# Reordered weight requests, column-tile runs, score slots and output products in a fused windowed-attention and gated feed-forward kernel

## The chip, the cores and the metric

The kernel runs on one core of one Trainium2 chip. The metric is the device time of one execution, in microseconds (us). The time before is the median of three runs.

The core's engines are named as in the profile: PE is TensorE (matrix products), PEld its weight loads, ACT ScalarE, DVE VectorE, POOL GpSimd, SP SyncE. SP, ACT and POOL also ask for transfers. All engines run side by side, each through its own list of instructions in order, and wait for one another by semaphores.

## What is computed

Attention in which each query sees the first four keys ("sinks") and the last 128, and then a gated feed-forward layer on the joined heads.

```python
batch, n_heads, seq, head_dim = (4, 8, 768, 64);  n_sink, window = (4, 128)
scores = scale * np.matmul(q, k.transpose(0, 1, 3, 2))
keep = is_sink | in_window
a = softmax(np.where(keep, scores, -1e9))          # shortened
x = np.matmul(a, v)          # heads joined: 3072 tokens x 512
gate = np.maximum(x @ w_gate, 0.0)                 # 512 x 1536
val = x @ w_val                                    # 512 x 1536
out = gate * val @ w_out                           # 1536 x 512
```

All inputs and the output are float32 in memory. The kernel computes in bfloat16 and sums in float32.

## The kernel before

The kernel treats the four batches one after the other, and for each batch four pairs of heads. A pair of heads in a batch is a unit; units 0 to 3 are batch 0, units 4 to 7 batch 1, and so on. The work of TensorE is laid out in 96 slots, 24 for each batch. A slot holds one chunk of the feed-forward layer: four products for the gate and four for the value, for one of 12 column tiles m of 128, and for one of two halves g of the batch's tokens.

```python
for ko in range(KO):                                  # 4: the gate, L356
    nc.tensor.matmul(out=gp[:, 0:n], lhsT=wg[:, ko, m * 128:(m + 1) * 128], rhs=x[:, ko, c], ...)
nc.scalar.activation(gs[:, 0:n], gp[:, 0:n], Act.Relu, ...)                       # L359
for ko in range(KO):                                  # the value, L361
    nc.tensor.matmul(out=vp[:, 0:n], lhsT=wv[:, ko, m * 128:(m + 1) * 128], rhs=x[:, ko, c], ...)
nc.vector.tensor_tensor(h[:, m, c], gs[:, 0:n], vp[:, 0:n], op=Alu.mult)          # L363
```

Batch 0 goes through its chunks in two runs: tiles 0 to 8 of half 0, then of half 1, then tiles 9 to 11 of both. The other batches have a single run of 12 tiles for each half.

```python
for b, runs in enumerate((((0, 9), (9, FM)),) + ((((0, FM),),) * (B - 1))):
    slots += [(b, g, m) for m0, m1 in runs for g in range(2) for m in range(m0, m1)]
```

After its chunk, a slot has pieces of attention of the same or the next batch, named by letters and a unit in the plans:
- T (L254 to L259): the casted keys and queries of a unit are turned on TensorE, copied out of PSUM, and the keys of the odd tiles are copied once more beside them (L185, and the four sink keys, L181). H is the same for half a unit of batch 0.
- S (L290, L294, L296): scores of one of three groups of key tiles, the exponential on ScalarE, and the mask on VectorE.
- W (L321, L326, L327): probabilities times V, and the division by the sum.
- X (L338, L341): the result is turned into xT, the input of the chunks.

For batches 2 and 3, T and X are done by transfers instead: cast, write to memory, and a transposing read back.

The second product of the feed-forward layer (L388) follows in pieces: one output tile of 128 tokens takes 12 products, one for each column tile. They all go to PSUM bank G[3] until the tail, where three banks rotate. After the twelfth, ScalarE copies the tile out (L392).

```python
OP = [[G[3][:]], [G[3][:], PP[0][:, 0, :], PP[1][:, 0, :]]]
...
nc.tensor.matmul(out=op, lhsT=hT[b % 2][:, m, t * 128:(t + 1) * 128], rhs=wo[:, m, :], start=m == 0, stop=m == FM - 1)
if m == FM - 1:
    ot = outpool.tile([128, d_model], F32, name="ot")
    nc.scalar.copy(ot[:], op)                                                     # L392
    nc.sync.dma_start(out=out[...], in_=ot[:])
```

The list of these products is filled at the end of slot 23. Slot 23 takes some of them at once (F8 and F5 in its plan: 13), and each later slot takes three:

```python
for _ in range(3 if s > 23 else 0):
    if f2:
        f2.popleft()()
```

Weights are asked for from GpSimd, with a cast to bfloat16 on the way: `load_w(m0, m1)` asks for tiles m0 to m1 of both weights, `load_w(m0, m1, (1,))` for those of w_val alone. GpSimd also casts keys, queries and V to bfloat16, and does so in the order of the program. `prep[s]` lists what is given to GpSimd and SyncE ahead of slot s: ("half", c) and ("kq", i) cast keys and queries, ("v", b, j) casts one tile of V, ("load", i) asks for a unit's keys and queries (for units 4 to 6 only once ScalarE has come to that slot), ("lv", b) for a batch's V, ("w", ...) and ("wo",) for weights.

```python
prep[1] += [("half", 6), ("half", 7), ("w", 6, 8), ("setup3",), ("v", 0, 3), ("v", 0, 4), ("v", 0, 5), ("v", 0, 6),
            ("w", 8, 10)]
prep[7] += [("load", 4), ("load", 5), ("load", 6)]
prep[9] += [("kq", 4), ("load", 7), ("lv", 1)]
prep[10] += [("kq", 5), ("w", 10, 12)]
prep[12] += [("kq", 6)]
prep[13] += [("kq", 7)]
prep[14] += [("v", 1, 0), ("v", 1, 1), ("v", 1, 2), ("v", 1, 3), ("wo",), ("v", 1, 4), ("v", 1, 5), ("v", 1, 6)]
```

Of the kernel before, what the change touches and what calls it, by code (L numbers as in the profile page):

```python
# [21 lines left out]
def kernel(  # L22
# [12 lines left out]
    nc = tc.nc  # L35
    B, H, S, D = q.shape
# [5 lines left out]
    FM = d_ff // 128  # L42
# [65 lines left out]
    half = lambda bufs, c: bufs[c // 2 % len(bufs)][:, c % 2 * HALF:c % 2 * HALF + HALF]  # L108
# [7 lines left out]
    def cast_half(c, copies=(nc.gpsimd.tensor_copy, nc.gpsimd.tensor_copy)):  # L116
        for src, dst, copy in ((kf, kn, copies[0]), (qf, qn, copies[1])):
            copy(half(dst, c).rearrange("p (n h d) -> p h n d", n=3, h=2),
                                  half(src, c).rearrange("p (h n d) -> p h n d", n=3, h=2))
# [13 lines left out]
    def cast_v(b, j, rows=128, copy=nc.gpsimd.tensor_copy):  # L133
        copy(vn[b % 2][0:rows, j, :, 0:64], vf[0:rows, j, :, :])  # L134
# [44 lines left out]
    def sinks(u, copy):  # L179
        e = kE[u.i % NT]  # L180
        copy(odd(e)[:, :, 0:4], e[:, 0:4].unsqueeze(1).to_broadcast([128, 3, 4]))  # L181

    def odd_tiles(u, copy):
        e = kE[u.i % NT]
        copy(odd(e)[:, :, 4:128], e[:, 120:876].rearrange("d (i c) -> d i c", c=252)[:, :, 0:124])  # L185
        sinks(u, copy)

    def load_w(m0, m1, which=(0, 1)):
        for w, dst in (((moe_w_gate, wg), (moe_w_val, wv))[x] for x in which):
            nc.gpsimd.dma_start(out=dst[:, :, m0 * 128:m1 * 128],  # L190
                                in_=w.rearrange("(ko ki) n -> ki ko n", ki=128)[:, :, m0 * 128:m1 * 128])
# [47 lines left out]
    def pair():  # L239
        rot[0] += 1  # L240
        return PP[rot[0] % 2]
# [6 lines left out]
    def T(u):  # L248
        t = u.i % NT
        tk, tq = G[3][:], pair()[:, 0, :]  # L250
        for x, ps in ((kn[u.i % 2], tk), (qn[u.i % 2], tq)):
            for n in range(NR):
                c = slice(128 * n, 128 * n + 128)
                nc.tensor.transpose(ps.bitcast(BF16)[:, c], x[:, c], ident[:])  # L254
        vk, vq = (ps.bitcast(BF16)[:, 0:S].rearrange("d (n p) -> d p n", p=128) for ps in (tk, tq))
        e = kE[t]
        to = lambda ap: ap.rearrange("d (p n) -> d p n", n=NR)
        nc.scalar.copy(to(e[:, 0:S]), vk)
        (nc.scalar.copy if u.p < 2 else nc.vector.tensor_copy)(to(qT[t]), vq)  # L259
        odd_tiles(u, nc.vector.tensor_copy)  # L260

    def T_half(c, banks=None):
        t, x = c % NP, c // NP
        tk, tq = banks or (G[3][:, 0:256], G[3][:, 256:512])
        for src, ps in ((kn, tk), (qn, tq)):
            for n in range(3):
                nc.tensor.transpose(ps.bitcast(BF16)[:, 128 * n:128 * n + 128], half(src, c)[:, 128 * n:128 * n + 128],  # L267
                                    ident[:])
        vk, vq = (ps.bitcast(BF16)[:, 0:HALF].rearrange("d (n p) -> d p n", p=128) for ps in (tk, tq))
        e = kE[t]  # L270

        for r0, r1, c0 in (((0, 128, 0), (40, 82, ODD + 4), (124, 128, ODD + 140)) if x == 0 else
                           ((0, 128, HALF), (0, 38, ODD + 152), (80, 122, ODD + 276))):
            nc.scalar.copy(e[:, c0:c0 + 3 * (r1 - r0)].rearrange("d (p n) -> d p n", n=3), vk[:, r0:r1])  # L274
        (nc.scalar.copy if c == 4 else nc.vector.tensor_copy)(
            qT[t][:, x * HALF:x * HALF + HALF].rearrange("d (p n) -> d p n", n=3), vq)
        if x == 0:
            sinks(U[t], nc.scalar.copy)
# [116 lines left out]
    with tc.manual_schedule():  # L395
# [22 lines left out]
        Sg(U[1], 3)  # L418
        cast_half(3)
        T_half(3, (g[0], g[1]))  # L420
        for j in range(3):
            cast_v(0, j)
        load_w(0, 2, (1,))
        load_w(2, 4)
        Sg(U[2], 0)
        Sg(U[2], 3)
# [19 lines left out]

        slots = []

        for b, runs in enumerate((((0, 9), (9, FM)),) + ((((0, FM),),) * (B - 1))):
            slots += [(b, g, m) for m0, m1 in runs for g in range(2) for m in range(m0, m1)]  # L450
        plan = [[] for _ in slots]
        at = {}
# [1 line left out]
        def put(s, y, n):  # L454
            st = (y[0], n * NP + int(y[1]), int(y[2]) if len(y) > 2 else 0)
            at[st] = s
            plan[s].append(st)

        for s, w in {0: "H0", 1: "S04 H1", 2: "S02 H2 S14", 3: "S12 H3", 4: "S24 S22", 5: "S34 S32", 6: "W01",
                     7: "W11 X01 W21", 8: "X11 W31 X21 X31"}.items():  # L460
            for y in w.split():
                put(s, y, 0)
        for s, w in {11: "T0", 12: "T1", 13: "S00 S01", 14: "S02 S10", 15: "T2 S11", 16: "S12 T3", 17: "S20 S21",
                     18: "S22 W0", 19: "S30 X0", 20: "S31 W1", 21: "S32 X1", 22: "W2", 23: "W3 X2 F8 X3 F5"}.items():
            for y in w.split():
                if y[0] == "F":
                    plan[s].append(("F", int(y[1:]), 0))
                else:
                    put(s, y, 1)
        for b, sl in ((2, {25: "S00 S01", 27: "S02 S10", 29: "S11 S12", 31: "S20 S21", 32: "W0", 33: "S22 S30",  # L470
# [3 lines left out]
            for s, w in sl.items():  # L474
                for y in w.split():
                    put(s, y, b)
        prep = [[] for _ in slots]
        prep[1] += [("half", 6), ("half", 7), ("w", 6, 8), ("setup3",), ("v", 0, 3), ("v", 0, 4), ("v", 0, 5), ("v", 0, 6),
                    ("w", 8, 10)]
        prep[7] += [("load", 4), ("load", 5), ("load", 6)]  # L480
        prep[9] += [("kq", 4), ("load", 7), ("lv", 1)]
        prep[10] += [("kq", 5), ("w", 10, 12)]
        prep[12] += [("kq", 6)]
        prep[13] += [("kq", 7)]
        prep[14] += [("v", 1, 0), ("v", 1, 1), ("v", 1, 2), ("v", 1, 3), ("wo",), ("v", 1, 4), ("v", 1, 5), ("v", 1, 6)]
        for i, ts in ((8, (13, 17, 18, 20)), (9, (14, 18, 19, 21)), (10, (15, 20, 21, 23)), (11, (19, 21, 22, 25)),
                      (12, (28, 31, 33, 36)), (13, (30, 33, 35, 38)), (14, (32, 35, 37, 42)), (15, (34, 37, 39, 43))):
# [13 lines left out]
        for s, (b, g, m) in enumerate(slots):  # L501
# [38 lines left out]
            for what, i, x in plan[s]:  # L540
                if what == "F":
                    for _ in range(i):
                        f2.popleft()()
                elif what == "X":
                    X(U[i], x if i < NP else None)
                elif what == "T":
                    T(U[i])
                elif what == "H":
                    T_half(NP + i)
                elif what == "S":  # L550
                    Sg(U[i], x)
                else:
                    W(U[i], x if i < NP else None)
# [43 lines left out]
```

The softmax here doesn't subtract the row's maximum and nothing guards it: scores larger than these inputs give would overflow.

## Time and profile before

| | before |
|---|---|
| time, median of three runs | 280.89 us (280.35 to 284.46) |
| profiled run, and its span from first to last instruction | 286.93 us, 285.0 us |
| PE busy | 244.7 us (86%) |
| DVE, ACT, POOL busy | 120.9, 120.8, 67.9 us |
| mean granted clock of PE | 0.974 |
| moved by DMA | 40.07 MB, mean 141 GB/s |

How to read it: the span is shown in 40 slices of 7.1 us, with one digit for each engine, the busy share in tenths. PEclk is the clock granted to TensorE, in tenths of full speed. A wait line names an engine and line, then what released it, then the total of those waits in us, their number and the longest. A line of a timeline has start, length, engine, line, operation, tiles, shape and count, and in brackets the idle time before it and its releaser. An engine's idle time costs something only where other work then comes later, in the end the last instruction; here TensorE has by far the most work.

### The profile page before, as it was taken

Reading aid. Unit: us, or ns where it says so; the run is one execution under the profiler, and the core shown is the slowest. Engines: PE = TensorE matmul, PEld = TensorE weight load, DVE = VectorE, ACT = ScalarE, POOL = GpSimd, SP = SyncE. Lnnn points to the kernel's source line nnn. Section 1 sums busy time; section 2 is a strip of 40 time slices with the busy share of each in tenths; the row PEclk is TensorE's granted clock in tenths of the full one; section 3 lists DMA queues with packets and bytes.
Section 4 is the critical chain, followed back from the end, with each engine's and each line's share of the span. In section 5 each row is a group of like instructions: output and inputs, shape, how many; then the busy total and the mean of one; then the engine's idle time right before and its main releaser. Section 6 shows DMA issues by size and latency. Waiting matters only on the chain.

```text
span 285.0 us, 5299 instructions
## 1 busy us (share of the span) xinstructions
PE 244.7 (86%) x2063; PEld 141.4 (50%) x2084; DVE 120.9 (42%) x227; ACT 120.8 (42%) x222; POOL 67.9 (24%) x120
## 2 busy tenths in 40 slices
PE   7869825997899978879889988978998988988895
PEld 3445523565466544546444545545554444544443
DVE  5466830379665335564322544645222222222100
ACT  4748711497473546452223645442222322222221
POOL 6895433099252126023004400000000000000000
PEclk9999985899799999999999999999999999999999
DMA  7999599799999834599997410231411000010113
GB/s 221 256 238 185 106 286 292 161 317 212 284 220 192 193 94 166 173 276 207 173 224 172 94 39 37 62 96 36 112 48 39 37 37 3 37 38 37 39 74 110
DMA packets 76737, 40.07 MB, mean 141 GB/s; under 512 B 53544, under 2 KB 73768, under 8 KB 76712
## 3 DMA queue, kind: packets, MB, share of 16 engines
q1 hardware_dynamic: 67560, 34.10, 47.0%
q0 software_dynamic: 7920, 4.72, 11.8%
q10 hardware_dynamic: 1232, 0.92, 1.0%
q8 instruction: 16, 0.26, 0.4%
q14 instruction: 9, 0.07, 0.1%
HBM read 28.48 MB, written 11.25 MB: 139 GB/s over the span
## 4 chain that ended last, share of the span: by engine, by line
PE 67%; DMA 13%; ACT 7%; SPq 5%; DVE 4%; issue 3%; POOL 1%; ACTq 0%; POOLq 0%; DVEq 0%
PE g L361 19%; PE g L388 19%; PE g L356 18%; DMA vf<-in_v_dram 5%; DMA wv<-in_moe_w_val_dram 4%; ACT ot L392 4%; PE pp L321 4%; DMA qf<-in_q_dram 4%; PE pp L290 3%; SPq L131 3%; ACT ee L294 3%; PE pp L388 2%; DVE xn L327 1%; DVE ee L296 1%; SPq L113 1%
## 5 line engine op out<-in xcount | busy, mean ns | idle before, releaser
L363 DVE TENSOR_TENSOR hT<-gs,g 128x384 bf16<-128x384 f32 (+2 forms) x96 | 53.0, 552 | 116.7 <-PE g L361 112.9
L359 ACT ACTIVATE gs<-g 128x384 f32<-128x384 f32 (+2 forms) x96 | 47.6, 496 | 109.5 <-PE g L356 108.7
L356 PE MATMUL g<-xT,wg 128*128 128x384 bf16 (+2 forms) x384 | 79.7, 330 | 6.3 <-DMA wg<-in_moe_w_gate_dram 6.1
L361 PE MATMUL g<-xT,wv 128*128 128x384 bf16 (+2 forms) x384 | 79.4, 330 | 4.2 <-DMA wv<-in_moe_w_val_dram 4.2
L388 PE MATMUL g<-wo,hT 128*128 128x512 bf16 x232 | 65.6, 379 | 18.8 <-ACT ot L392 17.3
L356 PEld LDWEIGHTS <-wg 128*128 128x128 bf16 x384 | 36.3, 98 | 56.0 <-issue 21.8
L361 PEld LDWEIGHTS <-wv 128*128 128x128 bf16 x384 | 37.5, 99 | 31.5 <-DMA wv<-in_moe_w_val_dram 6.4
L294 ACT ACTIVATE ee<-pp 128x998 bf16<-128x998 f32 (+4 forms) x52 | 45.0, 907 | 13.7 <-PE pp L290 13.5
L296 DVE TENSOR_TENSOR ee<-ee,msk 128x838 bf16<-128x838 bf16 (+3 forms) x44 | 31.6, 721 | 15.7 <-ACT ee L294 15.2
L388 PEld LDWEIGHTS <-hT 128*128 128x128 bf16 x276 | 25.4, 98 | 24.6 <-issue 1.9
L134 POOL CAST vn<-vf 128x512 bf16<-128x512 f32 x28 | 17.8, 649 | 44.5 <-DMA vf<-in_v_dram 44.4
L166 POOL CAST kn<-kf 128x768 bf16<-128x768 f32 x12 | 10.7, 890 | 43.3 <-DMA kqd<-kn 15.5
L321 PEld LDWEIGHTS <-ee 128*128 128x128 bf16 x512 | 18.4, 99 | 3.3 <-issue 1.4
L290 PE MATMUL pp<-KQ 64*128 64x252 bf16 (+6 forms) x328 | 17.3, 225 | 2.4 <-DVE KQ L259 2.3
L392 ACT COPY ot<-g 128x512 f32<-128x512 f32 x21 | 12.3, 587 | 14.8 <-PE g L388 14.1
L290 PEld LDWEIGHTS <-KQ 64*128 64x128 bf16 x328 | 11.3, 95 | 13.8 <-issue 11.5
L321 PE MATMUL pp<-vn,ee 128*128 128x65 bf16 x464 | 17.3, 195 | 0.6 <-POOL vn L134 0.6
L327 DVE TENSOR_TENSOR xn<-pp,rn 128x896 bf16<-128x896 f32 (+1 forms) x16 | 15.9, 991 | 0.5
L166 POOL CAST qn<-qf 128x768 bf16<-128x768 f32 x12 | 10.4, 871 | 1.8 <-DMA qf<-in_q_dram 1.7
L341 ACT COPY xT<-g 128x396 bf16<-128x396 bf16 (+2 forms) x8 | 4.5, 560 | 8.0 <-PE g L338 8.0
L274 ACT COPY KQ<-g 128x384 bf16<-128x384 bf16 (+3 forms) x24 | 6.2, 345 | 3.0 <-PE g L267 3.0
L385 DVE COPY ot<-pp 128x256 f32<-128x256 f32 x1 | 0.4, 425 | 14.5 <-PE pp L382 14.5
(76 smaller groups left out, 117.7 us busy)
## 6 DMA issues: line engine op xcount, KB each, us to landing
out_dram<-ot SPq DMA_DIRECT2D x23, 256.0 KB
kf<-in_k_dram SPq DMA_DIRECT2D x12, 384.0 KB
qf<-in_q_dram SPq DMA_DIRECT2D x12, 384.0 KB
vf<-in_v_dram SPq DMA_DIRECT2D x12, 256.0 KB
vf<-in_v_dram SPq DMA_DIRECT2D x12, 224.0 KB
kf<-in_k_dram SPq DMA_DIRECT2D x8, 192.0 KB
wg<-in_moe_w_gate_dram POOLq DMA_DIRECT2D x6, 256.0 KB, 8.7
wv<-in_moe_w_val_dram POOLq DMA_DIRECT2D x6, 256.0 KB, 10.2
```

What stands on the lines that cost most here:

```text
L166: nc.gpsimd.tensor_copy(dst[u.i % 2][:].rearrange("p (n h d) -> p h n d", n=NR, h=2), src[u.i % NQ][:].rearrange("p (h n d) -> p h n d", n ...
L290: nc.tensor.matmul(out=ps[:, h, c0:c1], lhsT=kE[t][64 * h:64 * h + 64, x0:x0 + 128], rhs=qT[t][64 * h:64 * h + 64, q0:q0 + c1 - c0], start ...
L294: nc.scalar.activation(x, ps[:, :, b0:n], Act.Exp, bias=0.0, scale=scale)
L296: nc.vector.tensor_tensor(x, x, msk[:, g, b0:n].unsqueeze(1).to_broadcast([128, 2, n - b0]), op=Alu.mult)
L321: nc.tensor.matmul(out=at[h][:, c:c + 65], lhsT=ee[u.i % NE][:, g, h, c0:c0 + 128], rhs=vn[u.b % 2][:, j, 2 * u.p + h, 0:65], start=c == 0 ...
L327: nc.vector.tensor_tensor(x.rearrange("p t (h d) -> p h t d", h=2), o[:, :, :, 0:64], r.unsqueeze(3).to_broadcast([128, 2, n, 64]), op=Alu ...
L356: nc.tensor.matmul(out=gp[:, 0:n], lhsT=wg[:, ko, m * 128:(m + 1) * 128], rhs=x[:, ko, c], start=ko == 0, stop=ko == KO - 1)
L359: nc.scalar.activation(gs[:, 0:n], gp[:, 0:n], Act.Relu, bias=0.0, scale=1.0)
L361: nc.tensor.matmul(out=vp[:, 0:n], lhsT=wv[:, ko, m * 128:(m + 1) * 128], rhs=x[:, ko, c], start=ko == 0, stop=ko == KO - 1)
L363: nc.vector.tensor_tensor(h[:, m, c], gs[:, 0:n], vp[:, 0:n], op=Alu.mult)
L388: nc.tensor.matmul(out=op, lhsT=hT[b % 2][:, m, t * 128:(t + 1) * 128], rhs=wo[:, m, :], start=m == 0, stop=m == FM - 1)
L392: nc.scalar.copy(ot[:], op)
```

## The change

It has four parts.
1. The first request for w_val goes ahead of three V casts on GpSimd; the request for tiles 6 and 7 goes behind one V cast but ahead of the three others, which wait for V; tiles 8 to 11 are asked for together, ahead of slot 9.
2. Batch 0 goes through tiles 0 to 7 of both halves and then through tiles 8 to 11 of both, so that tiles 8 to 11 are wanted later. The last W and X of batch 0's second half are packed into slots 6 and 7, since the second half of the tokens now begins at slot 8.
3. Batch 1's loads, casts, turns (T), scores (S) and W stand earlier, in another order. The copies of the odd keys in T go from VectorE to GpSimd.
4. Slot 23 takes 3 of the output products instead of 13; the other ten are left to the end.

```diff
-        odd_tiles(u, nc.vector.tensor_copy)
+        odd_tiles(u, nc.gpsimd.tensor_copy)
...
         T_half(3, (g[0], g[1]))
+        load_w(0, 2, (1,))
         for j in range(3):
             cast_v(0, j)
-        load_w(0, 2, (1,))
         load_w(2, 4)
...
-        for b, runs in enumerate((((0, 9), (9, FM)),) + ((((0, FM),),) * (B - 1))):
+        for b, runs in enumerate((((0, 8), (8, FM)),) + ((((0, FM),),) * (B - 1))):
...
         for s, w in {0: "H0", 1: "S04 H1", 2: "S02 H2 S14", 3: "S12 H3", 4: "S24 S22",
-                     5: "S34 S32", 6: "W01", 7: "W11 X01 W21", 8: "X11 W31 X21 X31"}.items():
+                     5: "S34 S32", 6: "W01 W11", 7: "X01 W21 X11 W31 X21 X31"}.items():
...
-        for s, w in {11: "T0", 12: "T1", 13: "S00 S01", 14: "S02 S10", 15: "T2 S11", 16: "S12 T3", 17: "S20 S21",
-                     18: "S22 W0", 19: "S30 X0", 20: "S31 W1", 21: "S32 X1", 22: "W2", 23: "W3 X2 F8 X3 F5"}.items():
+        for s, w in {9: "T0", 10: "T1", 11: "T2", 12: "S00 S01", 13: "S02 T3", 14: "S10 S11", 15: "S12", 16: "S20 S21",
+                     17: "S22 S30", 18: "S31 S32", 19: "W0", 20: "W1 X0", 21: "W2 X1", 22: "W3 X2", 23: "X3 F3"}.items():
...
-        prep[1] += [("half", 6), ("half", 7), ("w", 6, 8), ("setup3",), ("v", 0, 3), ("v", 0, 4), ("v", 0, 5), ("v", 0, 6),
-                    ("w", 8, 10)]
-        prep[7] += [("load", 4), ("load", 5), ("load", 6)]
-        prep[9] += [("kq", 4), ("load", 7), ("lv", 1)]
-        prep[10] += [("kq", 5), ("w", 10, 12)]
-        prep[12] += [("kq", 6)]
-        prep[13] += [("kq", 7)]
+        prep[1] += [("half", 6), ("half", 7), ("setup3",), ("v", 0, 3), ("w", 6, 8), ("v", 0, 4), ("v", 0, 5), ("v", 0, 6)]
+        prep[6] += [("load", 4), ("load", 5), ("load", 6)]
+        prep[8] += [("kq", 4), ("load", 7), ("lv", 1)]
+        prep[9] += [("kq", 5), ("w", 8, 12)]
+        prep[10] += [("kq", 6)]
+        prep[11] += [("kq", 7)]
```

More of the change, by code (lines that the diff above doesn't have):

```diff
@@ L457, in put @@
             plan[s].append(st)
-        for s, w in {0: "H0", 1: "S04 H1", 2: "S02 H2 S14", 3: "S12 H3", 4: "S24 S22", 5: "S34 S32", 6: "W01",
-                     7: "W11 X01 W21", 8: "X11 W31 X21 X31"}.items():
+        for s, w in {0: "H0", 1: "S04 H1", 2: "S02 H2 S14", 3: "S12 H3", 4: "S24 S22", 5: "S34 S32", 6: "W01 W11",
+                     7: "X01 W21 X11 W31 X21 X31"}.items():
             for y in w.split():
                 put(s, y, 0)
-        for s, w in {11: "T0", 12: "T1", 13: "S00 S01", 14: "S02 S10", 15: "T2 S11", 16: "S12 T3", 17: "S20 S21",
-                     18: "S22 W0", 19: "S30 X0", 20: "S31 W1", 21: "S32 X1", 22: "W2", 23: "W3 X2 F8 X3 F5"}.items():
+        for s, w in {9: "T0", 10: "T1", 11: "T2", 12: "S00 S01", 13: "S02 T3", 14: "S10 S11", 15: "S12", 16: "S20 S21",
+                     17: "S22 S30", 18: "S31 S32", 19: "W0", 20: "W1 X0", 21: "W2 X1", 22: "W3 X2", 23: "X3 F3"}.items():
             for y in w.split():
```

## The prediction, written before the result was known

> **What bounds the kernel now.** I read the page's busy shares and slices first, then the list of waits, then TensorE's timeline at the longest waits, then GpSimd's timeline and the DMA stages beside them.
>
> The page's parts 1 and 2 (share of the 285.0 us; slices of 7.1 us):
>
> ```profile
> PE 244.7 (86%) x2063; PEld 141.4 (50%) x2084; DVE 120.9 (42%) x227; ACT 120.8 (42%) x222; POOL 67.9 (24%) x120
> ...
> PE   7869825997899978879889988978998988988895
> ...
> PEclk9999985899799999999999999999999999999999
> DMA  7999599799999834599997410231411000010113
> ```
>
> TensorE (PE) is the engine that everything waits for; no other is over 42%. Its hole is in the sixth and seventh slices (2 and 5), with a lowered clock there (8, 5, 8) and again in slice eleven (7). From the eighth slice on it never falls below 7 until the last, so what is lost there is lost in small pieces. The list of waits (total us, times, longest) says which:
>
> ```profile
> PE g L388 <- ACT ot L392: 17.3, 20, 1.7
> ...
> PE g L356 <- DMA wg<-in_moe_w_gate_dram: 6.1, 1, 6.1
> ...
> PE g L361 <- DMA wv<-in_moe_w_val_dram: 4.2, 4, 2.1
> ...
> PE pp L290 <- DVE KQ L259: 2.3, 1, 2.3
> ```
>
> Together 29.9 us of TensorE standing still, in three kinds. TensorE's timeline (start, length, what, count, idle before) shows the weight wait, and what follows it:
>
> ```profile
> 36.94 0.77 PE L321 MATMUL pp<-vn,ee 128*128 128x65 bf16 x20
> 43.84 1.42 PE L356 MATMUL g<-xT,wg 128*128 128x372 bf16 x4 [6.13 <-DMA wg<-in_moe_w_gate_dram]
> 47.41 1.42 PE L361 MATMUL g<-xT,wv 128*128 128x372 bf16 x4 [2.15 <-DMA wv<-in_moe_w_val_dram]
> ```
>
> This is slot 8, column tile m = 8 of batch 0. Four products take 1.42 us instead of 0.80: the granted clock is 0.50 from 42.5 to 50 us. GpSimd's timeline says why the weights are late:
>
> ```profile
> 32.91 1.53 POOL L134 CAST vn<-vf 128x512 bf16<-128x512 f32 x2 [3.78 <-DMA vf<-in_v_dram]
> 34.39 0.74 POOL L190 DMA_DIRECT2D wg<-in_moe_w_gate_dram  x1
> 35.12 0.75 POOL L190 DMA_DIRECT2D wv<-in_moe_w_val_dram  x1
> ```
>
> The request stands in GpSimd's program behind casts that waited for V until 32.79, then lands beside 2.4 MB of keys and queries; the value half lands at 47.36 (12.2 us). The other kind is small and regular, again TensorE's timeline:
>
> ```profile
> 101.64 0.60 PE L388 MATMUL g<-wo,hT 128*128 128x512 bf16 x2
> 103.84 0.38 PE L388 MATMUL g<-wo,hT 128*128 128x512 bf16 x1 [1.60 <-ACT ot L392]
> 104.05 0.81 PE L356 MATMUL g<-xT,wg 128*128 128x384 bf16 x4
> ```
>
> A slot runs three output products. The end of an output tile falls after the second, and the third begins the next tile in the same bank, so TensorE waits for ScalarE's copy: 0.67 us, or 1.60 when exponentials queue ahead of the copy. The waits of 93 to 265 us alone give 15.9 us in 18 times, those of 265 to 285 another 1.3 in 2.
>
> **What the Trainium skill says.** Three places bear on it.
> - "TensorE: Matmul & The Clock Gate", Part 1 (the HAM clock gate): an idle window of about 3.4 us halves the clock, and about as much activity restores it. The trace agrees: 8.3 us of idle, then clock 0.50 until about 51.5 us.
> - "DMA: Bandwidth & Descriptors", Issuing engines are not separate DMA queues: requests of all engines share the same 16 DMA engines. So a weight request that leaves earlier takes time from others. The trace agrees: in the stage 20 to 26 us the weights' queue holds 86% and the other queue 48%.
> - "SBUF — State Buffer", SBUF: two separate sides: VectorE and GpSimd share a port pair as a lock. The trace agrees: the 12-element copy at L181 on VectorE takes 0.15 us alone and 0.73 to 0.78 while GpSimd casts; GpSimd's L185 copy takes 0.50, once 0.95.
>
> **The change part by part.**
>
> *Order of weights.* The first wv request moves ahead of three V casts (12.85 to about 10.1 us). That ends slot 0's wait of 1.19 us, but slot 2 waits for wv(2,4) until 24.03 in either kernel, and the DMA engines are full (share 1.2 to 1.36) from 5 to 30 us. I credit 0. Requests for m = 6, 7 move behind the memsets (2.8 us) and one V cast, from 20.1 to about 23.5. The weights' queue still has earlier tiles to move then, so they should land at about the same 32.8; slot 6 waits for them in both kernels. Again 0, with about 1 us of risk.
>
> *Runs of 8 and 4.* The first run ends at m = 7, whose weights have landed by 32.8. Tiles 8 to 11 are asked for in slot 9 (POOL at about 42 us) and used in slot 16, about 55 us. So the 6.1 and 2.15 us, and the slow clock after them, go. Absolute times: slot 6 ends at 33.5 as now, W01 and W11 run to 35, slot 7 to 36.3; then W21, W31 and four X in a chain of two rounds of PSUM read-out (0.2 + 0.7 us) and one copy of 0.5, until about 40.3. There slot 8, the first of the other column half, begins. Before, that point (slot 9) is 51.65.
>
> *Batch 1's turns and scores.* From there to the end of slot 23 the kernel before needs 41.5 us. The kernel after has one tile more (1.34) and 10 products fewer (13 to 3, at 0.217: 2.2). The 2.3 us wait, 1.4 of smaller ones and about 1.5 lost to the clock of 0.5 to 0.9 between 70 and 77 us should go, since turns now stand two to four slots ahead of the scores and no X follows its W at once. 41.5 + 1.3 − 2.2 − 5.2 = 35.4. ScalarE's own sum for the same stretch: slots 9 to 18 hold ten ReLUs of 0.5, twelve exponentials (mean 0.96) and six copies of 0.8, 21.4 us, against TensorE's ten tiles of 1.34, score products of about 3.7 and four turns of 0.67, 19.8. So ScalarE may hold it up by 1 to 1.5. I take 36.5 us: slot 24 begins at 40.3 + 36.5 = 76.8 instead of 93.2, **16.4 us sooner**.
>
> *Odd keys on GpSimd.* It takes four pairs of copies, 4.5 us as measured in the crowded stage, from VectorE and adds 4 x (0.5 + 0.19) = 2.8 us to GpSimd. What matters is the order: a copy stands behind the next unit's casts, which wait for DMA. Units 4 to 7's scores start one slot or more later; I count it inside the 36.5.
>
> *Products moved.* With 3 instead of 13 done before slot 24, tile ends fall on slot ends: 3, 6, 9, 12. The next tile's first product then has a whole tile of the gate and value products (1.30 us) ahead of it, which covers copy and hand-over (0.67). Only slots 50 and 54 have two exponentials ahead of the copy; there 1.30 + 0.65 stands against about 2.2, leaving 0.25 each. Saved: 15.9 − 0.5 + 1.3 in the tail, where three banks already rotate. Added: ten products at the end, 2.2. Net **14.5 us**.
>
> *What then comes nearer.* Batch 2's keys go through memory and back while the DMA engines are busy. Before, keys of units 8 to 11 are complete at about 83, 88, 101 and 111 us, and used at 96.5, 101, 112 and 119: 8 to 14 us of slack. SyncE cannot ask for them much sooner, since V of batch 1 holds its queue until about 56 us in both; I put their completion 5 to 8 us sooner, their use 16 to 21 sooner. That eats the slack. I allow 2.5 us.
>
> The sum: 285.0 − 16.4 − 14.5 + 2.5 = 256.6 us of span. The profiled run took 286.9, 6 more than the median of 280.89, and nearly all that can vary lies before 93 us, in waits for DMA that go. So I may not take the whole 28.4 off 280.89: 252.5 if the surplus stays elsewhere, 256.6 + 1.9 (run less span) = 258.5 if all of it was in the wait. I say 256.
>
> **The rivals.**
> 1. *Transfers become the bound.* The weight wait only turns into waits for U6's and U7's loads, batch 1's V, or batch 2's keys. For it: the DMA share is above 1 nearly all the way from 35 to 90 us, and the saving moves every use sooner. Against: they lie idle from 32.5 to 35, half idle from 52 to 55, and again from 100 to 105. If right, 5 to 9 us come back and the clock drops with them: 262 to 266.
> 2. *ScalarE and VectorE become the bound* in slots 12 to 18, with two scores per slot: 2.4 us of ScalarE against 2.0 of TensorE. It would cost 2 to 4 us more: about 259.
> 3. *The boundary waits only move.* If the copy still comes behind ScalarE's other work, the next tile waits after its chunk instead. Against: in most slots ScalarE is idle over half of the time. If right, only half of the 15.9 goes: 263.
> 4. *All of it was already hidden.* Against: the waits are TensorE's own, and the chain of waits passes through it for 67% of the span.
>
> **Range and chances.** Both large terms are waits read off TensorE. To lose the 2% both would have to fail nearly whole. With all stalls of rival 1 I reach 264, with none and the lower start 250.
>
> **What would show it.** No wait for wg over 2 us on TensorE and no clock of 0.5 after 15 us; slot 24's first gate product near 77 us; L388's wait for L392 under 2 us in total; the last turn's odd keys of batch 2 ahead of their scores. The prediction is wrong if TensorE shows waits for KQ, vn or wv between 30 and 100 us of over 5 us, if the slots from 12 to 18 take 2.5 us each or more with ScalarE full, or if L388 still waits at tile ends.

## The result, and the profile after

The kernel after takes 257.74 us (median of four, 256.96 to 259.0) against 280.62: the ratio is 0.9224, 95% interval 0.9128 to 0.932. The ratios in this document leave out executions more than 1.5% slower than the fastest of the same kernel, here one of 284.46 us of the kernel before. The profiled run has a span of 255.0 us. 256 was predicted, within 250 to 264.

The page of the kernel after, parts 1 and 2 (busy us and share of the span; then 40 slices of 6.4 us):

```profile
PE 241.3 (95%) x2084; PEld 140.6 (55%) x2084; DVE 118.4 (46%) x219; ACT 120.4 (47%) x222; POOL 69.7 (27%) x126
...
PE   7887988999896999999999999999999999999994
...
PEclk9999999999999799999999999999999999999999
DMA  7999969989999999899999502334210011110232
```

TensorE's busy time is nearly the same (244.7 before), its share rises from 86 to 95%. The hole in slices six and seven is gone, and from slice fourteen on every slice but the last is a 9. In the fourteenth a clock of 7 is new. The list of waits (total us, times, longest):

```profile
PE g L338 <- DVE xn L327: 2.0, 3, 1.2
PE pp L290 <- DMA KQ<-kqd: 1.5, 1, 1.5
PE g L361 <- DMA wv<-in_moe_w_val_dram: 1.3, 1, 1.3
...
PE pp L290 <- POOL KQ L181: 0.9, 2, 0.5
...
PE g L388 <- ACT ot L392: 0.2, 1, 0.2
```

No wait for wg is left, the 17.3 us at tile ends have become 0.2, and there are two new lines for KQ: the scores of batch 2 wait for keys that come back from memory. TensorE's timeline (start, length, what, count, idle before) at the new wait, and after it at the end of an output tile, where the kernel before could wait 1.60 us:

```profile
78.05 0.81 PE L361 MATMUL g<-xT,wv 128*128 128x384 bf16 x4
80.39 0.28 PE L290 MATMUL pp<-KQ 64*128 64x244 bf16 x2 [1.53 <-DMA KQ<-kqd]
81.09 0.53 PE L290 MATMUL pp<-KQ 64*128 64x252 bf16 x10 [0.42 <-POOL KQ L181]
81.55 0.82 PE L388 MATMUL g<-wo,hT 128*128 128x512 bf16 x3
82.21 1.29 PE L356 MATMUL g<-xT,wg 128*128 128x384 bf16 x4
83.29 1.48 PE L361 MATMUL g<-xT,wv 128*128 128x384 bf16 x4
84.57 1.43 PE L388 MATMUL g<-wo,hT 128*128 128x512 bf16 x3
85.83 0.81 PE L356 MATMUL g<-xT,wg 128*128 128x384 bf16 x4
86.49 0.81 PE L361 MATMUL g<-xT,wv 128*128 128x384 bf16 x4
87.23 0.61 PE L290 MATMUL pp<-KQ 64*128 64x252 bf16 x14
87.78 0.82 PE L388 MATMUL g<-wo,hT 128*128 128x512 bf16 x3
```

The first output tile ends with the three products at 84.57 (3 in slot 23, then 3 in each slot). The next tile begins in the same bank at 87.78, behind a whole chunk and two scores, and waits for nothing. The new wait has a price beyond its 1.95 us: four gate products take 1.29 us at 82.21, and 0.81 again from 85.83.

A table by stage makes the rest easy. Slot 24 is the first of batch 1's chunks; its first gate product parts the program in two. The second profile of the kernel before is that of "The kernel before again" below.

| start to slot 24, from there to the end, span (us) | to slot 24 | from slot 24 | span |
|---|---|---|---|
| before, first profile | 93.2 | 191.8 | 285.0 |
| before, second profile | 86.6 | 193.4 | 280.0 |
| after | 75.4 | 179.6 | 255.0 |

### The profile page after: what moved, and what is told of

It is laid out like the page before. It is cut to its first block, busy times and chain, and to the rows that moved or that the text cites. A ratio compares the mean times of both kernels' runs of the same rounds, so it can differ in the third digit from the quotient of the medians.

```text
span 255.0 us, 5316 instructions
## 1 busy us (share of the span) xinstructions
PE 241.3 (95%) x2084; PEld 140.6 (55%) x2084; DVE 118.4 (46%) x219; ACT 120.4 (47%) x222; POOL 69.7 (27%) x126
## 4 chain that ended last, share of the span: by engine, by line
PE 73%; DMA 12%; DVE 5%; ACT 4%; issue 3%; POOL 1%; ACTq 0%; SPq 0%; DVEq 0%; POOLq 0%
PE g L361 20%; PE g L356 20%; PE g L388 20%; PE pp L321 5%; DMA wv<-in_moe_w_val_dram 4%; PE pp L388 3%; PE pp L290 3%; DMA vf<-in_v_dram 3%; DVE ee L296 3%; ACT ee L294 3%; DMA KQ<-kqd 3%; DMA qf<-in_q_dram 2%; PE g L338 1%; DVE xn L327 1%; DVE hT L363 1%
## 5 line engine op out<-in xcount | busy, mean ns | idle before, releaser
L388 PE MATMUL g<-wo,hT 128*128 128x512 bf16 x240 | 64.6, 382 | 0.3 <-ACT ot L392 0.2
L296 DVE TENSOR_TENSOR ee<-ee,msk 128x838 bf16<-128x838 bf16 (+3 forms) x44 | 33.2, 765 | 17.4 <-ACT ee L294 16.9
L388 PEld LDWEIGHTS <-hT 128*128 128x128 bf16 x276 | 25.6, 98 | 24.1 <-issue 1.3
L134 POOL CAST vn<-vf 128x512 bf16<-128x512 f32 x28 | 18.8, 685 | 34.5 <-DMA vf<-in_v_dram 34.4
L392 ACT COPY ot<-g 128x512 f32<-128x512 f32 x20 | 11.7, 587 | 21.6 <-PE g L388 21.6
L321 PEld LDWEIGHTS <-ee 128*128 128x128 bf16 x512 | 17.7, 97 | 2.2 <-issue 0.3
L321 PE MATMUL pp<-vn,ee 128*128 128x65 bf16 x464 | 16.4, 193 | 0.0
L185 POOL COPY KQ<-KQ 128x372 bf16<-128x372 bf16 x12 | 6.9, 575 | 6.4 <-ACT KQ L258 4.3
L388 PE MATMUL pp<-wo,hT 128*128 128x512 bf16 x36 | 8.1, 379 | 0.0
```

Source lines behind the costliest of these rows:

```text
L296: nc.vector.tensor_tensor(x, x, msk[:, g, b0:n].unsqueeze(1).to_broadcast([128, 2, n - b0]), op=Alu.mult)
L321: nc.tensor.matmul(out=at[h][:, c:c + 65], lhsT=ee[u.i % NE][:, g, h, c0:c0 + 128], rhs=vn[u.b % 2][:, j, 2 * u.p + h, 0:65], start=c == 0 ...
```

## The experiments

**Output products: number or remainder.** Four runs in one session, with a median of 279.95 us for the kernel before in it. First, this part of the change alone, on the kernel before:

```diff
-22: "W2", 23: "W3 X2 F8 X3 F5"
+22: "W2", 23: "W3 X2 F3 X3"
```

> The kernel before with one edit: slot 23 takes 3 output products instead of 13. Theory (the end of an output tile now falls on a slot's end, so ScalarE's copy hides behind the next chunk): the 15.9 us of L388 waiting for L392 between slots 24 and 95 fall to under 1 us, and the median goes down by 13 to 15 us, to about 267 us. Rival (the waits only move to the next chunk or the next tile): at most half of that, 273 us or more. Weight wait and slow clock of slot 8 stay as they are.

Measured: 268.05 us median. The profiled run took 263.43, and its list of waits has 0.2 us for L388 on L392; slot 24 begins at 86.3 and 175.4 us follow, 16.4 less than in the first profile of before. That one run, 16.5 us below the median of before, fits the 17 us of waits that went. The three others took 268.06, 268.05 and 268.97, and have no profile; why they are 5 us slower stays open. What follows: the waits go, and not half of them moves elsewhere; all four lie under the rival's 273.

Next, everything but this part: the kernel after with `23: "X3 F13"`.

> The kernel after with one edit: slot 23 takes 13 products, as before. Theory: all of the other parts of the change stay, the waits of L388 for L392 come back with 14 to 16 us, and the median is about 271 us (258 + 14). Rival (the ten products left to the end are what matters, or the copies hide anyway): within 2 us of 258.

Measured: 275.22 us, ratio to before 0.9851 (0.9766 to 0.9936). Its list of waits:

```profile
PE g L388 <- ACT ot L392: 17.3, 20, 1.7
PE pp L290 <- POOL KQ L181: 1.8, 1, 1.8
```

The whole 17.3 us are back. So all other parts of the change together are worth some 5 us at the end, and this one, added to them, some 17.5.

Is it the ten products left over, or where the tile ends fall? With `F6` they fall on slot ends again, with `F5` they don't.

> The kernel after with 6 products in slot 23 instead of 3. Tile ends still fall on slot ends. Theory (only the remainder by 3 counts): within 1 us of 258, waits of L388 for L392 under 1 us. Rival (the number left to the end counts): 0.7 us off for each 3, and a change of the waits in proportion.

> The kernel after with 5 products in slot 23. A tile then ends after the first product of a slot, and the next tile's first product follows at once. Theory: the waits come back as with 13, 0.67 us or more for each of 18 tiles, 12 to 16 us in all, and the median is 270 to 274 us. Rival (number, not remainder): within 1 us of 258.

Measured: 256.75 us with 6 (ratio 0.9204, 0.9124 to 0.9284), 274.52 us with 5 (0.9738, 0.9624 to 0.9853). The same line of the two lists of waits, first with 6, then with 5:

```profile
PE g L388 <- ACT ot L392: 0.2, 1, 0.2
```

```profile
PE g L388 <- ACT ot L392: 14.9, 18, 1.9
```

One product more makes some 15 us by the two ratios, and 14.7 in this line. The waits go with the remainder by three and not with the number, as expected.

**The weight request alone.** The kernel before, runs of 9 and 3 kept, with one request moved:

```diff
-("v", 0, 3), ("v", 0, 4), ("v", 0, 5), ("v", 0, 6), ("w", 8, 10)]
+("v", 0, 3), ("w", 8, 10), ("v", 0, 4), ("v", 0, 5), ("v", 0, 6)]
```

> The kernel before with one edit: the weight request for tiles 8 and 9 goes ahead of the three V casts that wait, directly after the cast of V's tile 3, everything else as before (runs of 9 and 3). Theory (the wait in slot 8 comes from the request's place in GpSimd's program alone): it leaves at about 25 instead of 34 us, slot 8 waits under 1 us instead of 6 to 8, and the median falls by 5 to 9 us, to 272 to 276. Rival (the transfers are full until 31 us, so the earlier request delays V, or the weights still land at 38 or later): 0 to 3 us less.

Measured: 274.96 us, within the expected range; by the ratio, 0.9827 (0.9749 to 0.9905), that is 4.8 us less, just under the 5 to 9. GpSimd's timeline in it:

```profile
24.53 0.64 POOL L134 CAST vn<-vf 128x512 bf16<-128x512 f32 x1
25.08 0.76 POOL L190 DMA_DIRECT2D wg<-in_moe_w_gate_dram  x1
25.81 0.77 POOL L190 DMA_DIRECT2D wv<-in_moe_w_val_dram  x1
28.21 0.61 POOL L134 CAST vn<-vf 128x512 bf16<-128x512 f32 x1 [1.63 <-DMA vf<-in_v_dram]
```

The request leaves at 25 us, and TensorE's slot 8 runs through without a wait:

```profile
38.31 0.79 PE L356 MATMUL g<-xT,wg 128*128 128x372 bf16 x4
38.94 0.79 PE L361 MATMUL g<-xT,wv 128*128 128x372 bf16 x4
```

The V casts behind it cost TensorE one wait of 0.94 us. The second half of the tokens begins at 41.8 us, against 39.1 in the kernel after, where one tile (1.3 us) less stands ahead of it. So the wait came from the request's place in GpSimd's program; the runs of 8 are one way to be rid of it, not the only one. In time this one move (0.9827) brings as much as all parts of the change but the output products together (0.9851 above). There slot 24 begins 4.6 us sooner than here (77.3 against 81.9), but 195.3 us follow it instead of 191.8.

**The kernel before again**, for a second profile.

> The kernel before once more, for a second profile of it. Theory (the 6 us by which the first profile lies over the median are in the transfers' waits before slot 24): the first half-slot product of slot 24 begins at 84 to 89 us instead of 93.2, and from there to the end it takes 191 to 193 us again. Rival (the surplus is spread): slot 24 at 91 to 93.

Measured: 281.95 us, span 280.0. TensorE's timeline at slot 8:

```profile
37.77 0.80 PE L356 MATMUL g<-xT,wg 128*128 128x372 bf16 x4 [0.40 <-DMA wg<-in_moe_w_gate_dram]
42.44 1.42 PE L361 MATMUL g<-xT,wv 128*128 128x372 bf16 x4 [3.87 <-DMA wv<-in_moe_w_val_dram]
```

4.3 us of waiting for these weights where the first profile had 8.3, and slot 24 at 86.6. The rest, 193.4 us, is 0.4 above the expected range; the clock was 0.91 and 0.92 between 100 and 120 us. So what sets the two profiles apart lies before slot 24 (6.6 us less there, 1.6 more behind it).

**Batch 1's plan and the odd keys.** The next three runs were taken with the kernel after itself as their base.

> The kernel after without an edit, as the base for the runs beside it on the same chip: 257 to 259 us.

Measured: 256.92 us, from 256.27 to 259.2 in six runs, ratio 0.9185 (0.9124 to 0.9245). First the old plan for slots 11 to 23 in the kernel after:

```diff
-{9: "T0", 10: "T1", 11: "T2", 12: "S00 S01", 13: "S02 T3", ... 22: "W3 X2", 23: "X3 F3"}
+{11: "T0", 12: "T1", 13: "S00 S01", 14: "S02 S10", 15: "T2 S11", ... 22: "W2", 23: "W3 X2 F3 X3"}
```

> The kernel after with the kernel before's plan of turns, scores, W and X of batch 1 in slots 11 to 23 (3 products kept). Theory of the prediction (turns two to four slots ahead of the scores and no X right after its W take away waits of TensorE between slots 11 and 23): a wait for the queries' copy comes back, slot 24 begins 2 to 4 us later, the median rises by 2 to 4 us. Rival (that wait came from the stall and the crowding of VectorE before, not from the plan, and later keys of batch 2 would hide the shift): within 1 us.

Measured: 257.74 us (256.48 to 259.28). Slot 24 begins at 80.2 us, 5 to 6 later than in the two profiles of the kernel after, with a wait of 2.95 us for odd keys. But only 177.0 us follow, against 179.6 and 180.1. About half of what the new plan brings by slot 24 is given back behind it in the profiles, and the ranges of the runs overlap: a gain in time from the plan is not shown. The rival was right about the time, though a wait did come, for the odd keys and not for the queries' copy.

Then the odd keys on VectorE again (`odd_tiles(u, nc.vector.tensor_copy)` in T).

> The kernel after with the odd keys' copies of batch 1's turns back on VectorE. Theory A (VectorE is the engine that TensorE waits for in slots 15 to 20, and GpSimd's copies relieve it): VectorE does 2 to 4.5 us more there, slot 24 begins 1 to 2 us later, the median rises by 0 to 2 us. Theory B (the copies lie before that stretch, where VectorE has room, and GpSimd is the one that holds up the casts): no rise, or 0.5 us less. Either way below 1% of the time.

Measured: 258.08 us (255.83 to 258.9); slot 24 at 75.3, as with GpSimd. The ranges overlap; whether it matters which engine copies batch 1's odd keys can't be told from these runs.

**The new wait.** Batch 2's first scores one slot later (`26: "S00 S01"` instead of 25):

> The kernel after with the first scores of batch 2 (unit 8, two groups) in slot 26 instead of 25. Theory (the new wait of 1.5 and 0.4 us for the keys read back from memory, and the half clock for 3.4 us that follows it, are due to the scores coming too soon): the wait goes below 0.3 us, the clock stays at 1.0, and the median falls by 2 to 3.5 us. Rival (the wait only shifts to unit 9's scores in slot 27, or the exponentials then delay the copy of the tile that ends in slot 26): within 1 us.

Measured: 256.78 us (256.07 to 258.42). The wait for the read back went and the clock stayed at 1.0, as the theory had it, but the time is the rival's: now units 9 and 10 wait for L181, 3.7 us in two times. All of batch 2 two slots later:

```diff
-(2, {25: "S00 S01", 27: "S02 S10", 29: "S11 S12", ... 37: "W2", 38: "W3"})
+(2, {27: "S00 S01", 29: "S02 S10", 31: "S11 S12", ... 39: "W2", 40: "W3"})
```

> The kernel after with all scores and W of batch 2 two slots later (slots 27 to 40 instead of 25 to 38). Theory (the remaining waits of 2 to 5 us for KQ, in slots 25 to 31, come from the keys' way through memory, and the slots have room until 48): no wait for KQ over 0.3 us, the clock stays at 1.0, the median falls by 3 to 4 us to about 253.5. Rival (W's or the later read back of xT then becomes late, or the exponentials fall on tile ends): within 1 us of the kernel after.

Measured: 257.16 us (256.34 to 258.6). The theory fails for the wait that is left: it is one for L181, and not for the keys' way through memory. TensorE's timeline, then GpSimd's, in this kernel:

```profile
87.73 0.84 PE L290 MATMUL pp<-KQ 64*128 64x252 bf16 x10 [2.57 <-POOL KQ L181]
```

```profile
82.33 0.62 POOL L134 CAST vn<-vf 128x512 bf16<-128x512 f32 x1 [1.49 <-DMA vf<-in_v_dram]
86.48 0.62 POOL L134 CAST vn<-vf 128x512 bf16<-128x512 f32 x1 [3.54 <-DMA vf<-in_v_dram]
87.04 0.50 POOL L185 COPY KQ<-KQ 128x372 bf16<-128x372 bf16 x1
87.48 0.19 POOL L181 COPY KQ<-KQ 128x12 bf16<-128x12 bf16 x1
```

The copy at 87.04 waits for no transfer of its own (no idle time before it); it stands in the program behind a cast that waited 3.54 us for V. Moving the scores moved the copies behind more such casts. The kernel after itself has the same at unit 10, in slot 31; GpSimd's timeline, then TensorE's:

```profile
95.85 0.62 POOL L134 CAST vn<-vf 128x512 bf16<-128x512 f32 x1 [2.43 <-DMA vf<-in_v_dram]
96.41 0.50 POOL L185 COPY KQ<-KQ 128x372 bf16<-128x372 bf16 x1
96.85 0.19 POOL L181 COPY KQ<-KQ 128x12 bf16<-128x12 bf16 x1
```

```profile
97.10 0.53 PE L290 MATMUL pp<-KQ 64*128 64x252 bf16 x10 [0.49 <-POOL KQ L181]
```

So the copies of batch 2 were given to the other engine, at the same places:

```diff
-odd_tiles(U[x[1]], nc.gpsimd.tensor_copy)
+odd_tiles(U[x[1]], nc.vector.tensor_copy if x[1] < 12 else nc.gpsimd.tensor_copy)
```

> The kernel after with the odd keys' copies of batch 2 (units 8 to 11) on VectorE instead of GpSimd, at the same places in the program. Theory A (the second of the KQ waits, in slot 31, comes from the copy standing behind casts of V on GpSimd that wait for a transfer): that wait goes, 1 to 2.6 us less, median about 255.5. Theory B (the read back itself lands late): VectorE waits for it and holds up the gate-and-value products' read-out behind it; no gain, or 1 to 3 us lost.

Measured: 255.25 us as the median of five executions from 254.96 to 256.08 (a sixth took 1368.78 us), ratio to before 0.9133 (0.908 to 0.9186). All five lie below every run of the kernel after (256.27 at least), and below all six of the run just before, on the same chip. Against the kernel after's 0.9185 that is some 1.5 us, with intervals that overlap. VectorE's timeline at the first and third of the four copies:

```profile
80.16 0.29 DVE L185 COPY KQ<-KQ 128x372 bf16<-128x372 bf16 x1 [1.21 <-DMA KQ<-kqd]
80.36 0.16 DVE L181 COPY KQ<-KQ 128x12 bf16<-128x12 bf16 x1
...
94.62 0.28 DVE L185 COPY KQ<-KQ 128x372 bf16<-128x372 bf16 x1
```

There is no wait of TensorE for KQ in its list. From slot 24 to the end it takes 174.9 us, 4.7 less than the kernel after, though its slot 24 began late in this profile (79.1; TensorE waited 1.93 us for wg at slot 6). A later slot 24 gives the keys more time too: unit 8's were there at 80.2 us and wanted only at 82.5, so that the 174.9 are not the copies' doing alone. For unit 10 the lateness is not the reason. With the old plan, slot 24 began later still (80.2), and with the copies on GpSimd unit 10 waited:

```profile
99.44 0.53 PE L290 MATMUL pp<-KQ 64*128 64x252 bf16 x10 [1.39 <-POOL KQ L181]
```

Theory A holds for unit 10, the one it was about. This version has the lowest median here.

## Why the prediction was right, and where its terms were off

- **What bounds.** TensorE, and its own waits: right. Its busy time stayed at 241 to 245 us and its idle time fell.
- **Products moved: 14.5 us net, and so 16.7 of waits, predicted; 17.1 of waits went.** The mechanism held in each run: 17.3 us with remainder 1, 14.9 with remainder 2, 0.2 with 0. The residual in slots 50 and 54 was 0.2, not 0.5. The 2.2 us for ten products were charged here and credited before slot 24, so they cancel in the sum.
- **To slot 24: 16.4 us predicted, 11.1 between the second profile of before and the kernel after** (17.8 from the first). The absolute times were close: slot 8 at 39.1 (40.3 predicted), slot 24 at 75.4 (76.8). What was mis-sized is the base: the step "slot 24 begins at 40.3 + 36.5 = 76.8 instead of 93.2" took the 93.2 of one profile, whose weight wait was twice that of the second. The text gave this as the reason not to take the whole 28.4 off 280.89, and that saved the total.
- **Batch 1's plan: 36.5 us predicted for slots 8 to 23, 36.3 measured.** With the old plan they took 40.3, so in these profiles the plan brings 4.0 of the 5.2 us credited to it by slot 24; behind it half of that is lost again. ScalarE did not become the bound: slots 12 to 18 took 14.7 us together, 2.1 each. But VectorE held up one X by 1.15 us. Masks that take 0.60 to 0.69 us with GpSimd idle took 1.1 on average between 58 and 65 us, while GpSimd cast V and keys beside them; this agrees with the shared port pair quoted in the prediction.
- **Batch 2's keys: 2.5 us allowed, 4 to 5 given back.** The kernel after needs 179.6 and 180.1 us from slot 24, and 174.9 to 175.4 are seen where no such wait is. The waits were 2.4 and 4.6 us, and in the first case a half clock for 3.4 us. What was mis-sized is the step "I put their completion 5 to 8 us sooner": the last copies of units 8 to 10 ended 1.9, 1.5 and 4.1 us sooner. GpSimd's timeline, first before (units 8, 9, 10), then after (8 and 9; 10 is shown above):

```profile
82.72 0.19 POOL L181 COPY KQ<-KQ 128x12 bf16<-128x12 bf16 x1
88.11 0.19 POOL L181 COPY KQ<-KQ 128x12 bf16<-128x12 bf16 x1
100.92 0.19 POOL L181 COPY KQ<-KQ 128x12 bf16<-128x12 bf16 x1
```

```profile
80.84 0.19 POOL L181 COPY KQ<-KQ 128x12 bf16<-128x12 bf16 x1
86.61 0.19 POOL L181 COPY KQ<-KQ 128x12 bf16<-128x12 bf16 x1
```

The reason given, that V of batch 1 holds SyncE's queue until about 56 us, held (55.8), and for unit 8 the read back itself landed late. But for unit 10 the cause is the copies' place behind V's casts on GpSimd, an order that the prediction had named for batch 1 alone. Unit 9's copies stand there too; that its wait in the second profile (0.73 us) comes from this was not tested.

- **Odd keys on GpSimd** were counted inside the 36.5. No run shows a gain from them in batch 1.
- **Order of the weights: 0 credited.** The first profiles agree: slot 2 waited for wv until 23.6, and slot 6's value products began at 32.8 (released by ScalarE, not by the weights), both within 0.5 us of before. Between the second profiles slot 6's begin 1.4 us sooner (31.9 against 33.3), so a small gain is not ruled out.
- **Rivals.** The first came in part, on another engine than supposed. The other three did not.
- **Signs of being wrong.** Two came true in part, though the total held. A clock of 0.5 came back after 82 us, and in the second profile of the kernel after the waits for KQ and wv between 30 and 100 us sum to 5.2 us, where over 5 was named.
- **One reading was off.** "8.3 us of idle, then clock 0.50" is not the order in the trace: the clock fell to 0.5 at about 41.2 us, within the first wait, after some 3.5 us of idle.

The two parts nearly add up by the profiled run: with 13 products kept, the rest brings 4.7 us, the output products alone bring 16.5 (11 to 12 in the three other executions, which stay unexplained), and both together 22.9. The 1.7 us by which the time lies over the predicted 256 are of the size by which the keys of batch 2 were under-counted; that these are the same microseconds was not shown.

## What to carry to other kernels

Where a steady loop takes k small products per step from a row of n, with one PSUM bank, make the end of the row fall on the end of a step (n a multiple of k, and the first step aligned): the copy then hides behind the next step's other work, if that is longer (here 1.30 us against 0.67). An instruction that waits for a transfer holds up everything behind it on its engine, requests and copies that wait for nothing among them; put those ahead, or on another engine. Before sizing a wait on a transfer, compare the profiled run's time with the median: here one profile lay 5 us above another, and the surplus was in the stage with the waits.

## What the runs showed of the hardware that was not expected

A short wait of TensorE was followed by half the clock in some runs, and a longer one in others was not. In the kernel after, the clock's windows around the new wait (length; PE, PEld, DVE, ACT, POOL busy; clock; DMA share; GB/s):

```profile
79.00:81.00 2.00, 0.28 (x2) 0.10 (x2) 0.52 (x1) 0.00 (x0) 1.34 (x3) 1.00 1.32 241
81.00:82.00 1.00, 0.91 (x13) 0.55 (x14) 0.00 (x0) 0.57 (x1) 0.54 (x2) 1.00 1.28 274
82.00:83.00 1.00, 1.00 (x6) 0.47 (x5) 0.53 (x1) 1.00 (x2) 0.11 (x1) 0.70 1.12 388
83.00:84.00 1.00, 1.00 (x5) 0.48 (x4) 0.78 (x2) 0.75 (x2) 0.00 (x0) 0.50 0.45 118
```

1.53 and 0.42 us of idle, with 0.28 us of work between them, were followed by a clock of 0.5 until 85.7. In the other profile of the same kernel, waits of 1.33, 0.42, 0.73 and 2.15 us between 77 and 97 us left it at 1.0 throughout. With all of batch 2 two slots later, 2.57 us of idle were followed by 0.5 until about 91 us; with its first scores one slot later, 2.63 us left it at 1.0. Each of these is shorter than the idle window of about 3.4 us that the prediction quotes, so the clock fell here after less idle time than that. What decides between the two stays open.
